# Attention, top-1 experts and a cosine layer in one kernel: a copy and a sum moved to ACT and POOL, sixteen weight loads moved ahead, ring slots renumbered

## The chip, the cores and the metric

One NeuronCore of a Trainium2 chip runs the whole program. The metric is the device time of one execution in microseconds (us). The engines are PE (matrix products), DVE, ACT and POOL (elementwise work), and SP, which here only issues transfers. PEld is the loading of PE's weights.

## The reference, cut to what matters

```python
def _attn_ref(q, k, v, g_norm):                    # 8 batches, 8 heads, 576 tokens, 64 wide
    kv = np.einsum('bhsd,bhse->bhde', k, v)
    out = np.einsum('bhsd,bhde->bhse', q, kv)
    rms = np.sqrt(np.mean(out * out, axis=-1, keepdims=True) + 1e-06)
    return (out / rms * g_norm).astype(np.float32)

def _moe_ref(x, expert_emb, tau, w1, w2):           # 4608 tokens x 512, 8 experts, hidden 1024
    ...                                             # one expert per token, gate_w its probability
    for e in range(E):
        h = np.maximum(x[mask] @ w1[e], 0.0)
        out[mask] = gate_w[mask, None] * (h @ w2[e])

def _moe2_ref(x, w_in, w_out):                      # 512 -> 2048 -> 512, weights in float64
    h = x @ w_in
    g = h * np.cos(h)
    return (g @ w_out).astype(np.float32)
```

## The kernel before

Every matrix product is made to float32's accuracy from three products of rounded parts: each operand is written as `hi` (a rounded copy, made by ACT) plus `lo` (the rest, made by DVE). The program has three stages, one after the other, and the order of the instructions on each engine is the order of the code.

**Attention** (0 to about 144 us) also finds each token's expert and scatters the tokens to DRAM by expert.

**Experts** (about 144 to 612 us). Tokens come in 16 chunks of 304, two an expert. A loop counts steps `g` from 0 to 129; step `g` is `c, f = divmod(g, 8)`: chunk `c`, eighth `f` of the hidden width. In a step PE does `layer1(c, f)` (L253) and `layer2` of two steps before (L274). Into the same steps other work is laid by hand:
- `split_piece` (L140 on ACT, L141 on DVE) turns an eighth of an expert's weights from `raw` into `hi` and `lo` in one of 12 ring slots. Which slot a piece gets is found by the loop at L101 to 107, and with it the earliest step for its split (`split_at`).
- `gate_x` works out the gates of a coming chunk in small DVE and ACT operations (L174 to L210, with four `gx` operations in step f = 3), and `turn_x` turns its tokens into `xT` (L227 on PE, L232 on ACT, L233 on DVE) in steps f = 3 to 6. A chunk's first `layer1` (f = 0) needs all four `xT`.
- `convert` turns the float64 weights of the last stage into float32, on DVE: four bit operations (L324 to L331), four sums (L455) and three splits (L365, to the tile `wa`, with copies by ACT, L364) for each set, 16 sets in all. How much of it goes into a step is a sum kept by hand: `spare` grows by `FULL` = 32 a step, less what `vector_work` counts of other work (12 for a split).

**The cosine layer** (about 602 us to the end). Nine blocks `b` of 512 tokens, eight steps each, `step(i)` with `b, q_ = divmod(i, 8)` for 256 hidden columns. A fast scheme of seven products instead of eight is used for both layers: a step has seven products of the first layer (`ha`, `hb`, L1124), whose sums (`one`, `five`, `two`) ACT copies and DVE adds up to `h`; the cosine and the parts of `h` made in the step before; and seven products of the second layer (L1137) with the `h` of two steps before, into the PSUM banks `a11`, `s2`, `a12`, `s3`, `a22`, `s1`. Weights of the first layer, and three of the second, are streamed by `feed` through nine slots (`wb`, `wa` and two in the ring), each load issued on SP when a product is done with a slot. The other four of the second layer (`KEPT`) stay in SBUF: those of q_ = 0 are in `wa` already, those of q_ = 1 to 7 are 28 loads made by `keep_one` (L533) into ring slots. Eight of them are issued at the end of the loop over the experts, the others one for every second `feed`.

In the first step after a block (`after` in `step`; eight times in the program) DVE sums the finished banks into the output tiles `o_sb`, of which `late_sum` does two out of bank `s1` (`o_s` in the trace), and POOL writes the rows out by token number (L1195). The first second-layer product of the new block that goes to bank `s1` is the last of that step.

Of the kernel before, what the change touches and what calls it, by code (L numbers as in the profile page):

```python
# [14 lines left out]
ALU = mybir.AluOpType  # L15
# [14 lines left out]
CH = 304  # L30
CP = 76
NRB = 12
# [4 lines left out]
def tile_kernel(ctx, tc, q, k, v, g_norm, emb, tau, w1, w2, w_in, w_out, out):  # L37
    nc = tc.nc
# [53 lines left out]
    NC = len(chunks)  # L92
# [7 lines left out]
    free_at = [-99] * 8 + [OPEN] * 4  # L100
    slot_of, earliest = [], []  # L101
    for p, (first, final) in enumerate(use):

        i = p - 4 if 12 <= p < 16 else min(range(NRB), key=lambda x: (free_at[x], x))
        slot_of.append(i)
        earliest.append(free_at[i] + 1)
        free_at[i] = final
# [35 lines left out]
    V = nc.vector  # L143
# [136 lines left out]
    def store_y(c):  # L280
        o = [P.yo.tile([128, CH], F32, name="yo", tag="yo") for _ in range(4)]
        for d in range(4):
            if "gate" in c:
                V.tensor_tensor(out=o[d], in0=c["y"][d][:, 0:CH], in1=c["gate"], op=ALU.mult)  # L284
            else:
                nc.scalar.activation(out=o[d], in_=c["y"][d][:, 0:CH], func=ACTF.Copy)

        def flush():
            by_pool = c["n"] < BY_POOL or c["n"] == NC - 1
            queue = nc.gpsimd if by_pool else nc.sync  # L290
            col = c["col"](mybir.EngineType.Pool if by_pool else mybir.EngineType.SP)
            queue.dma_start(out=perm[bass.ds(col, CH)].rearrange("(p r) -> p r", r=4), in_=c["rows"])
            for d in range(4):
                queue.dma_start(out=yT[d * 128:(d + 1) * 128, bass.ds(col, CH)], in_=o[d])

        return flush
# [189 lines left out]
    KEPT = (W11, W21, W22, V1)  # L486
# [42 lines left out]
    def keep_one():  # L529
        q_, j = keeping.pop(0)  # L530
        if j == 0:
            WOUT[q_] = ring(WO[q_ - 1])
        nc.sync.dma_start(  # L533
            out=WOUT[q_][:, :, j * 256:j * 256 + 256].bitcast(F32), in_=wo[q_, KEPT[j]].rearrange("p (a c) -> p a c", a=2)
        )
# [39 lines left out]
    if True:  # L575
# [62 lines left out]
        for i in range(2):  # L638
# [6 lines left out]
            out=ident, in_=ones, pattern=[[1, 128]], compare_op=ALU.is_equal, fill=0.0, base=0, channel_multiplier=-1  # L645
        )
        nc.gpsimd.affine_select(
            out=upper, in_=ones, pattern=[[1, 128]], compare_op=ALU.is_gt, fill=0.0, base=0, channel_multiplier=-1
# [11 lines left out]
        for i in range(2):  # L660
            nc.gpsimd.iota(
                out=nums[64 * i:64 * i + 64, :, 8], pattern=[[2 * S, 4]], base=i * S + 512, channel_multiplier=1
# [322 lines left out]
        for t in range(NTILE):  # L985
            j, b, r = where(t)
# [60 lines left out]
    if True:  # L1047
# [55 lines left out]
        G, Y, bank = {}, {}, {}  # L1103
# [61 lines left out]
        def copy(out, in_):  # L1165
            nc.scalar.activation(out=out, in_=in_, func=ACTF.Copy)  # L1166

        def add(out, x, y):
            V.tensor_tensor(out=out, in0=x, in1=y, op=ALU.add)  # L1169

        def sub(out, x, y):
            V.tensor_tensor(out=out, in0=x, in1=y, op=ALU.subtract)  # L1172

        def f32(x):
            return x.bitcast(F32)
# [26 lines left out]
        def halves(x):  # L1202
            return x.rearrange("p (t c) -> p t c", t=2)

        OUT = {}
# [10 lines left out]
            return p.tile([128, 512], F32, name=name, tag=name)[:, 0:256]  # L1216

        def late_sum(b, t, x):
            add(OUT[b][t][:, :, 256:512], halves(x), halves(bank[b, "s1"]))
            for th in range(2):  # L1220
                out_row(b, t, th)

# [35 lines left out]
        def step(i):  # L1258
            if i == NS + 1:
                return last_step()  # L1260
            new, prev, j = i < NS, 1 <= i <= NS, i - 2
            last = i - 1
            b, q_ = divmod(j, 8)
            done = j >= 0 and q_ == 7
            after = j >= 8 and q_ == 0
# [11 lines left out]
            def o(kind="o"):  # L1277
                return out_product(pe(kind)) if j >= 0 else None

            if new:  # L1280
                xa = bank_of("ha", i)
                xb = bank_of("hb", i)
                if i:
                    h1, h0 = (hp_.tile([128, 512], F32, name="h", tag="h") for _ in range(2))
                    one, five, two = (sn.tile([128, 256], F32, name=nm, tag=nm) for nm in ("one", "five", "two"))
# [5 lines left out]
            else:  # L1291
                xa = xb = None
# [43 lines left out]
            if prev:  # L1336
                sub(s24[:, 1], r0[:, 1], s24[:, 0])
                copy(hi0, r0)
                copy(hi13, s13)
                copy(hi24, s24)  # L1340
                sub(lo0, r0, f32(hi0))
            if after:
                add(OUT[b - 1][1][:, :, 0:256], halves(E1), halves(bank[b - 1, "a22"]))
# [3 lines left out]
            if not i:  # L1347
                interleave(1)
            o()
            if prev:  # L1350
                sub(lo13, s13, f32(hi13))
            if new:
                add(h1[:, 256:512], five, xa)
                turns_of(i, 1)
            if done:
                add(U2, E1, bank[b, "s2"])
            if after:
                late_sum(b - 1, 1, E1)
            if new:
                xb = bank_of("hb", i)  # L1360
            h(xb, True)
# [6 lines left out]
            if done:  # L1368
                OUT[b] = [op.tile([128, 2, 512], F32, name=f"o_sb{t}", tag=f"o_sb{t}") for t in range(2)]
                add(OUT[b][0][:, :, 0:256], halves(E1), halves(bank[b, "a12"]))  # L1370
            if after:
                late_sum(b - 1, 0, Y["acc"])
            if prev:
                sub(lo24, s24, f32(hi24))
            if new:
# [30 lines left out]
        for n in range(5, NC):  # L1406
            GATE_AT[8 * n - 14] = LOAD_AT[8 * n - 17] = n
        raw_of = lambda: P.raw.tile([128, 1024], F32, name="raw", tag="raw")
        spare, FULL, CARRY = 0, 32, 15

        def vector_work(c, f, splits):
            w = 4 + 12 * splits + (6 if c >= NC - 2 else 14 if c == 2 else 0) + (16 if f == 1 and c < 5 else 0)
# [4 lines left out]
        for g in range(NC * 8 + LAG):  # L1417
# [41 lines left out]
            if g == 8 * NC - 5:  # L1459
                feed()  # L1460
                feed()
            if 8 * NC - 1 <= g < 8 * NC + 1:
                for _ in KEPT:
                    keep_one()
            if g < OPEN:
                paused.clear()
                advance(8)
# [240 lines left out]
```

## Time and profile before

| what | value |
|---|---|
| median of 3 runs | 1357.23 us (1357.14 to 1366.95) |
| the profiled execution, its own time | 1357.04 us |
| its span, first to last instruction | 1355.5 us |
| busy in the span | PE 1302.9 us (96%), DVE 1102.2 (81%), ACT 846.2 (62%), POOL 175.4 (13%) |
| moved by DMA | 359.31 MB, mean 265 GB/s |
| mean granted TensorE clock | 0.995 |

The 1.5 us between span and time lie outside the first and last instruction. A busy share is a mean over stages: in most slices of the span PE is busy without a gap, and its idle time lies in the attention stage, at the passage from one stage to the next, and in short waits between.

### The profile page before, as it was taken

The numbers are of one execution on the slowest core, as the hardware profiler recorded it, in microseconds if no ns is written. First come the engines' busy times: TensorE is split into PE (matmuls) and PEld (weight loads), VectorE is DVE, ScalarE is ACT, GpSimd is POOL, SyncE is SP. The second block draws the span as 40 slices with busy tenths as digits, with TensorE's granted clock in tenths as the row PEclk, the third lists the DMA queues.
The fourth block names the chain that finished last, engine by engine and source line by source line (L and its number), as shares of the span: only waits on it lengthen the run. The fifth ranks groups of instructions, "written<-read, shape, count | busy, mean of one in ns | idle before, by whom it ended". The sixth has DMA issues, their size and how long they took to land.

```text
span 1355.5 us, 30321 instructions
## 1 busy us (share of the span) xinstructions
PE 1302.9 (96%) x10825; PEld 1279.5 (94%) x10825; DVE 1102.2 (81%) x2511; ACT 846.2 (62%) x1698; POOL 175.4 (13%) x286
## 2 busy tenths in 40 slices
PE   7998799999999999998999999999999999999997
PEld 6886799999999999998999999999999999999997
DVE  2567867788989888866889898888989889798876
ACT  4667454677666776545666666676666766666663
POOL 1234132113220000000001010000101001010101
PEclk9999999999999999999999999999999999999998
DMA  9999485788888798659998888888889889888884
GB/s 276 290 326 284 133 246 129 209 249 261 251 249 272 253 281 274 211 163 329 339 320 296 284 293 269 290 285 299 284 267 309 271 290 294 284 291 271 262 284 136
DMA packets 238102, 359.31 MB, mean 265 GB/s; under 512 B 26045, under 2 KB 114913, under 8 KB 236729
## 3 DMA queue, kind: packets, MB, share of 16 engines
q1 hardware_dynamic: 221480, 297.20, 69.3%
q0 software_dynamic: 16448, 60.08, 14.0%
q8 instruction: 89, 1.46, 0.4%
q14 instruction: 69, 0.56, 0.1%
q10 hardware_dynamic: 16, 0.02, 0.0%
HBM read 299.32 MB, written 57.89 MB: 264 GB/s over the span
## 4 chain that ended last, share of the span: by engine, by line
PE 66%; DVE 11%; issue 9%; DMA 5%; ACT 4%; SPq 3%; POOL 1%; POOLq 0%; ACTq 0%; DVEq 0%
PE ha L1124 12%; PE y L274 10%; PE hb L1124 9%; PE o_s L1137 9%; PE o_a L1137 9%; PE hps L253 7%; PE hb L1137 3%; PE xp L253 3%; DMA vr<-in_v 1%; DMA wa<-ws 1%; SPq L599 1%; DVE gx L180 1%; DVE ring L141 1%; DVE o_sb L1169 1%; ACT gx L174 1%
## 5 line engine op out<-in xcount | busy, mean ns | idle before, releaser
L274 PE MATMUL y<-h,ring 128*128 128x304 f32 x1536 | 235.8, 302 | 1.3 <-DVE yo L284 1.3
L274 PEld LDWEIGHTS y<-h,ring 128*128 128x128 f32 x1536 | 220.1, 188 | 1.7 <-ACT h L259 1.5
L253 PE MATMUL hps<-xT,ring 128*128 128x304 f32 x1152 | 182.8, 308 | 2.7 <-DVE xT L233 1.8
L253 PEld LDWEIGHTS hps<-xT,ring 128*128 128x128 f32 x1152 | 165.0, 190 | 4.1 <-DVE xT L233 2.2
L1092 ACT ACTIVATE u<-u,half_pi 128x512 f32<-128x512 f32 x142 | 102.3, 720 | 56.8 <-DVE u L1089 56.8
L1195 POOL DMA_INDIRECT out<-o_sb,perm_i x36 | 48.6, 1350 | 684.8 <-DVE o_sb L1169 576.5
L1086 ACT ACTIVATE u<-h 128x512 int32<-128x512 f32 x142 | 89.7, 632 | 71.0 <-DVE h L1169 65.0
L1089 DVE SCALAR_TENSOR_TENSOR u<-h,u 128x512 f32<-128x512 f32 x142 | 97.9, 689 | 24.8 <-ACT u L1086 22.9
L1137 PE MATMUL o_a<-ring,hi 128*128 128x256 f32 x568 | 107.9, 282 | 0.0
L141 DVE TENSOR_TENSOR ring<-raw,ring 128x1024 fp32r<-128x1024 f32 x72 | 87.8, 1219 | 21.3 <-ACT ring L140 20.6
L1166 ACT ACTIVATE hi<-u 128x512 fp32r<-128x512 f32 x142 | 88.6, 624 | 26.5 <-DVE u L1172 26.5
L1172 DVE TENSOR_TENSOR lo<-u,hi 128x512 fp32r<-128x512 f32 x142 | 96.9, 683 | 0.0
L259 ACT ACTIVATE h<-hps 128x304 fp32r<-128x304 f32 x96 | 40.3, 419 | 78.6 <-PE hps L253 74.5
L1137 PEld LDWEIGHTS o_a<-ring,hi 128*128 128x128 f32 x568 | 87.2, 189 | 0.0
L1166 ACT ACTIVATE hi<-h 128x256 fp32r<-128x256 f32 (+1 forms) x142 | 74.2, 522 | 19.6 <-PE o_a L1137 9.1
L1325 DVE TENSOR_TENSOR h<-h,u 128x512 f32<-128x512 f32 x71 | 49.0, 690 | 44.5 <-ACT u L1092 44.1
L1137 PE MATMUL o_a<-ring,lo 128*128 128x256 f32 x284 | 79.7, 281 | 0.0
L1172 DVE TENSOR_TENSOR lo<-h,hi 128x256 fp32r<-128x256 f32 (+1 forms) x142 | 78.2, 550 | 0.0
L140 ACT ACTIVATE ring<-raw 128x1024 fp32r<-128x1024 f32 x72 | 75.8, 1053 | 0.0
L1137 PE MATMUL o_s<-ring,hi 128*128 128x256 f32 x376 | 71.9, 283 | 0.0
L253 PE MATMUL xp<-xT,ring 128*128 128x304 f32 x384 | 60.1, 303 | 2.4 <-DVE xT L233 2.4
L260 DVE SCALAR_TENSOR_TENSOR h<-hps,h 128x304 fp32r<-128x304 f32 x96 | 44.4, 463 | 18.2 <-ACT h L259 16.3
(333 smaller groups left out, 3374.2 us busy)
## 6 DMA issues: line engine op xcount, KB each, us to landing
wb<-ws SPq DMA_DIRECT2D x224, 256.0 KB
wa<-ws SPq DMA_DIRECT2D x167, 256.0 KB
raw<-in_moe_w SPq DMA_DIRECT2D x144, 256.0 KB
ring<-ws SPq DMA_DIRECT2D x113, 256.0 KB
wb<-wo SPq DMA_DIRECT2D x96, 256.0 KB
ring<-wo SPq DMA_DIRECT2D x75, 256.0 KB
wa<-wo SPq DMA_DIRECT2D x73, 256.0 KB
wo<-wa SPq DMA_DIRECT2D x52, 256.0 KB
```

The source lines that it names most:

```text
L140: nc.scalar.activation(out=w[:, 0], in_=raw, func=ACTF.Copy)
L141: nc.vector.tensor_tensor(out=w[:, 1], in0=raw, in1=w[:, 0].bitcast(F32), op=ALU.subtract)
L253: nc.tensor.matmul(out=p[:, 0:CH], lhsT=w[:, a, k * 128:(k + 1) * 128], rhs=c["xT"][b_][k], start=(n == 0), stop=(n == 11),)
L274: nc.tensor.matmul(out=c["y"][d][:, 0:CH], lhsT=w[:, a, 512 + d * 128:512 + (d + 1) * 128], rhs=h[b_], start=(f == 0 and i == 0), stop=(f ...
L1086: nc.scalar.activation(out=n, in_=p, func=ACTF.Copy, scale=TURN, bias=0.25)
L1089: V.scalar_tensor_tensor(out=u, in0=p, scalar=TURN, in1=n, op0=ALU.mult, op1=ALU.subtract)
L1092: nc.scalar.activation(out=u, in_=u, func=ACTF.Sin, scale=2 * math.pi, bias=half_pi)
L1124: nc.tensor.matmul(out=out, lhsT=w[:, a, k * 128:(k + 1) * 128], rhs=x[xi][:, b_, k * 256:(k + 1) * 256], start=(start and n == 0), stop=( ...
L1137: nc.tensor.matmul(out=o[:, th * 256:th * 256 + 256], lhsT=G[j, name][a][:, th * 128:th * 128 + 128], rhs=w[:, b_, 0:256], start=(start an ...
L1166: nc.scalar.activation(out=out, in_=in_, func=ACTF.Copy)
L1172: V.tensor_tensor(out=out, in0=x, in1=y, op=ALU.subtract)
L1325: V.tensor_tensor(out=r0, in0=r0, in1=two_of(Y["u", 0]), op=ALU.mult)
```

## The change

It has six parts:
1. **Ring slots.** Pieces 16 to 23 get slots 0 to 7. Their splits move: pieces 16 to 21 from steps 14, 16, 18, 20, 22, 24 to 19, 21, 22, 23, 24, 25; from piece 22 on the steps are as before. The last expert's pieces lie in slots 0 to 7 instead of 4 to 7 and 0 to 3.
2. **`FULL`** goes from 32 to 33.
3. **Kept weights.** Sixteen of the 28 loads (q_ = 1 to 4) are issued in steps 124, 125 and 126, instead of eight in steps 127 and 128; the other twelve stay with the feeds.
4. **Last chunk's output.** Of its four copies out of PSUM ACT keeps two, and DVE does two.
5. **Order of two DVE operations** in every step: `h1[:, 256:512]` is added ahead of the split `lo13`.
6. **`late_sum`.** ACT copies bank `s1` to `U2` behind `hi24`, and POOL adds `U2` for both output halves (`E1` and `Y["acc"]`), both in the place of the first; DVE no longer does these two sums.

```diff
-        i = p - 4 if 12 <= p < 16 else min(range(NRB), key=lambda x: (free_at[x], x))
+        i = p - 4 if 12 <= p < 16 else p - 16 if 16 <= p < 24 else min(range(NRB), key=lambda x: (free_at[x], x))
...
             if "gate" in c:
                 V.tensor_tensor(out=o[d], in0=c["y"][d][:, 0:CH], in1=c["gate"], op=ALU.mult)
+            elif c["n"] == NC - 1 and d % 2:
+                V.tensor_copy(out=o[d], in_=c["y"][d][:, 0:CH])
             else:
...
         def late_sum(b, t, x):
-            add(OUT[b][t][:, :, 256:512], halves(x), halves(bank[b, "s1"]))
+            nc.gpsimd.tensor_tensor(out=OUT[b][t][:, :, 256:512], in0=halves(x), in1=halves(U2), op=ALU.add)
             for th in range(2):
                 out_row(b, t, th)
...
                 copy(hi24, s24)
+                if after:
+                    copy(U2, bank[b - 1, "s1"])
                 sub(lo0, r0, f32(hi0))
...
+            if new:
+                add(h1[:, 256:512], five, xa)
             if prev:
                 sub(lo13, s13, f32(hi13))
             if new:
-                add(h1[:, 256:512], five, xa)
                 turns_of(i, 1)
             if done:
                 add(U2, E1, bank[b, "s2"])
             if after:
                 late_sum(b - 1, 1, E1)
+                late_sum(b - 1, 0, Y["acc"])
...
-            if after:
-                late_sum(b - 1, 0, Y["acc"])
...
-        spare, FULL, CARRY = 0, 32, 15
+        spare, FULL, CARRY = 0, 33, 15
...
-            if 8 * NC - 1 <= g < 8 * NC + 1:
-                for _ in KEPT:
-                    keep_one()
+            for _ in range({8 * NC - 4: 8, 8 * NC - 3: 4, 8 * NC - 2: 4}.get(g, 0)):
+                keep_one()
```

Three places show how instructions move. First SP at the passage from the experts to the cosine layer (steps 124 to 129), where loads from `ws` and those from `wo` into `wb` and `wa` are feeds, and the loads from `wo` into a numbered `ring` of 128x2x256 are kept weights. Before:

```order
L517 DMA wa<-ws 128x512 x3
L517 DMA ring_8090<-ws 128x512 x2
L533 DMA ring_8563<-wo 128x2x256
L517 DMA wb<-ws 128x512 x2
L533 DMA ring_8563<-wo 128x2x256
L517 DMA wb<-ws 128x512 x2
L533 DMA ring_8563<-wo 128x2x256
L517 DMA wa<-ws 128x512
L533 DMA ring_8563<-wo 128x2x256
L533 DMA ring_8671<-wo 128x2x256 x4
L533 DMA ring_8676<-wo 128x2x256 x3
L517 DMA wa<-ws 128x512 x2
```

And now, from the same three feeds on:

```order
L519 DMA wa<-ws 128x512 x3
L535 DMA ring_8464<-wo 128x2x256 x4
L535 DMA ring_8469<-wo 128x2x256 x4
L535 DMA ring_8503<-wo 128x2x256 x4
L535 DMA ring_8542<-wo 128x2x256 x4
L519 DMA ring_8097<-ws 128x512 x2
L519 DMA wb<-ws 128x512 x4
L519 DMA wa<-ws 128x512 x3
```

All sixteen stand ahead of the feeds of step 0 (two in the ring, four in `wb`, one in `wa`), and nothing stands between these and the next feeds to `wa`.

Second DVE in the first step after the first block (`o_sb` are output tiles, `o_s` the bank `s1`, `e` is `E1`; `u` and `h` the parts of the hidden layer). Before:

```order
L1172 TENSOR_TENSOR lo_10063<-h,hi_10062 128x512
L1169 TENSOR_TENSOR o_sb_10008<-e_8724,o_a_8955 128x2x256
L1172 TENSOR_TENSOR lo_10067<-u_9987,hi_10066 128x512
L1169 TENSOR_TENSOR h<-five,ha 128x256
L1169 TENSOR_TENSOR o_sb_10008<-e_8724,o_s_8965 128x2x256
L1169 TENSOR_TENSOR h<-one,hb 128x256
L1089 SCALAR_TENSOR_TENSOR u_10149<-h,u_10149 128x512
L1169 TENSOR_TENSOR o_sb_10007<-acc,o_s_8965 128x2x256
L1172 TENSOR_TENSOR lo_10069<-u_10049,hi_10068 128x512
L1188 TENSOR_TENSOR h<-h,u_10149 128x512
```

And now:

```order
L1174 TENSOR_TENSOR lo_10063<-h,hi_10062 128x512
L1171 TENSOR_TENSOR o_sb_10008<-e_8730,o_a_8960 128x2x256
L1171 TENSOR_TENSOR h<-five,ha 128x256
L1174 TENSOR_TENSOR lo_10067<-u_9987,hi_10066 128x512
L1171 TENSOR_TENSOR h<-one,hb 128x256
L1091 SCALAR_TENSOR_TENSOR u_10150<-h,u_10150 128x512
L1174 TENSOR_TENSOR lo_10069<-u_10049,hi_10068 128x512
L1190 TENSOR_TENSOR h<-h,u_10150 128x512
```

The two sums out of `o_s` are gone from DVE (POOL does them now, each in front of its two row writes), and the split of 128x512 stands behind the sum to `h` instead of in front of it.

Third DVE in steps 57 and 58 of the experts (`sb` and `sa` are the sums of the conversion, `wa` its splits). Before:

```order
L141 TENSOR_TENSOR ring_5119<-raw,ring_5119 128x1024
L326 SCALAR_TENSOR_TENSOR c_t<-c_raw,c_t 128x512
L329 SCALAR_TENSOR_TENSOR c_t<-c_raw,c_t 128x512
L331 SCALAR_TENSOR_TENSOR sa<-c_mk,c_t 128x512
L260 SCALAR_TENSOR_TENSOR h_5144<-xp,h_5143 128x304
L455 TENSOR_TENSOR sb<-sa 128x256
L455 TENSOR_TENSOR sa<-sa 128x256
L455 TENSOR_TENSOR sb<-sb,sa 128x256
L455 TENSOR_TENSOR sb<-sa,sb 128x256
```

And now:

```order
L141 TENSOR_TENSOR ring_5128<-raw,ring_5128 128x1024
L457 TENSOR_TENSOR sb<-sb,sa 128x256
L457 TENSOR_TENSOR sb<-sa,sb 128x256
L260 SCALAR_TENSOR_TENSOR h_5151<-xp,h_5150 128x304
L367 TENSOR_TENSOR wa<-sa,wa 128x2x256 x2
L367 TENSOR_TENSOR wa<-sb,wa 128x3x256
```

The conversion runs some operations ahead of where it ran, so its three splits, which need three copies by ACT, now fall into step 58 (f = 2) instead of step 60.

## Rows read from the trace of the kernel before

**Rows 1.** Waits of PE over the whole span: total us, how often, longest.
```profile
PE o_s L1137 <- DVE o_sb L1169: 4.0, 8, 0.5
PE xp L253 <- DVE xT L233: 2.4, 4, 0.7
```

**Rows 2.** Stretches: length, busy us (instructions) of PE, PEld, DVE, ACT, POOL, clock, DMA share, GB/s.
```profile
600.00:610.00 10.00, 10.00 (x80) 10.00 (x79) 3.42 (x7) 2.88 (x7) 0.00 (x0) 1.00 0.57 175
620.00:630.00 10.00, 7.36 (x50) 7.19 (x49) 6.61 (x14) 5.47 (x12) 0.00 (x0) 0.83 1.04 362
```

**Rows 3.** PE at the passage, in order of time: start, us, what, idle before and releaser.
```profile
614.63 0.98 PE L1124 MATMUL ha<-ring,ring 128*128 128x256 f32 x6 [1.04 <-ACT one L1166]
...
618.79 0.98 PE L1124 MATMUL ha<-ring,wb 128*128 128x256 f32 x6 [0.89 <-DVE h L1169]
...
624.55 1.20 PE L1124 MATMUL o_s<-ring,wa 128*128 128x256 f32 x6 [2.64 <-DMA wa<-ws]
...
635.19 0.95 PE L1124 MATMUL hb<-ring,wa 128*128 128x256 f32 x6 [0.79 <-DMA wa<-ws]
```

**Rows 4.** SP's queue at the passage, in order of time.
```profile
610.46 6.28 SPq L533 DMA_DIRECT2D ring<-wo  x8
616.85 1.45 SPq L517 DMA_DIRECT2D wa<-ws  x2
```

**Rows 5.** ACT and DVE at the passage, in order of time.
```profile
612.66 1.34 ACT L286 ACTIVATE yo<-y 128x304 f32<-128x304 f32 x4
617.11 1.29 DVE L1172 TENSOR_TENSOR lo<-raw,hi 128x512 fp32r<-128x512 f32 x2
622.03 0.36 ACT L1166 ACTIVATE one<-o_s 128x256 f32<-128x256 f32 x1
```

**Rows 6.** The second block's end and the step behind it, in order of time.
```profile
795.91 0.63 ACT L1086 ACTIVATE u<-h 128x512 int32<-128x512 f32 x1 [1.50 <-DVE h L1169]
...
800.62 0.36 ACT L1166 ACTIVATE one<-ha 128x256 f32<-128x256 f32 x1
...
801.03 0.98 PE L1124 MATMUL ha<-ring,wa 128*128 128x256 f32 x6
...
803.79 0.41 DVE L1169 TENSOR_TENSOR h<-two,hb 128x256 f32<-128x256 f32 x1
...
804.70 0.88 PE L1124 MATMUL hb<-ring,ring 128*128 128x256 f32 x6
```

**Rows 7.** POOL's elementwise sums, grouped by form over the whole span.
```profile
L878 POOL TENSOR_TENSOR exc<-exc,ohc 128x8 f32<-128x8 f32 x16 | 3.3, 209 | 6.9 <-DVE ohc L873 6.3
...
L865 POOL TENSOR_TENSOR w<-w,tie 128x24 f32<-128x24 f32 x8 | 2.0, 254 | 32.7 <-DVE w L864 32.6
```

**Rows 8.** DVE and POOL at 117 us, in order of time.
```profile
117.20 1.21 DVE L141 TENSOR_TENSOR ring<-raw,ring 128x1024 fp32r<-128x1024 f32 x1
117.28 1.20 POOL L879 TENSOR_TENSOR run<-exc,ohc 128x8 f32<-128x8 f32 x1
```

**Rows 9.** Experts: splits in steps 43 and 51, first products of steps 48 and 56.
```profile
308.73 1.23 DVE L141 TENSOR_TENSOR ring<-raw,ring 128x1024 fp32r<-128x1024 f32 x1 [0.47 <-ACT ring L140]
...
320.52 1.56 PE L253 MATMUL xp<-xT,ring 128*128 128x304 f32 x10
...
322.70 0.54 PE L253 MATMUL xp<-xT,ring 128*128 128x304 f32 x2 [0.63 <-DVE xT L233]
...
336.38 1.23 DVE L141 TENSOR_TENSOR ring<-raw,ring 128x1024 fp32r<-128x1024 f32 x1 [0.47 <-ACT ring L140]
...
349.43 1.94 PE L253 MATMUL xp<-xT,ring 128*128 128x304 f32 x12
...
399.70 0.69 DVE L326 SCALAR_TENSOR_TENSOR c_t<-c_raw,c_t 128x512 int32<-128x512 int32 x1
```

**Rows 10.** The split of step 14 on DVE, and PE's wait for a gate behind it.
```profile
202.05 1.22 DVE L141 TENSOR_TENSOR ring<-raw,ring 128x1024 fp32r<-128x1024 f32 x1 [0.37 <-ACT ring L140]
...
215.18 1.92 PE L274 MATMUL y<-h,ring 128*128 128x304 f32 x12 [1.29 <-DVE yo L284]
```

## The prediction, made before the changed kernel ran

> **What bounds the kernel now.** I began with the table of engines and went on to the list of waits. PE is busy 1302.9 of 1355.5 us, so nothing here pays unless it takes away an idle moment of PE, a stretch of low clock, or adds one. The list of waits by sum [rows 1] names two that the change touches: eight at the block boundaries of the cosine layer, 4.0 us in all, in which the last product of a step waits for DVE to empty bank `s1`, and four at the start of an expert's chunk, 2.4 us. The timeline adds four waits at the passage from the experts to the cosine layer [rows 3], 1.04 + 0.89 + 2.64 + 0.79 = 5.36 us, and the table of stretches shows there a granted clock of 0.83 for 10 us [rows 2]: PE had been held up just before, and the chip granted only part of full speed. One more wait, 1.29 us, lies early in the experts [rows 10]. All together about 15 us stand within reach, 1.1% of the time. The page's sum is made against the profiled execution, 1357.04 us; the median is 0.2 us above it, which I neglect.
>
> **Passage (parts 3, 4 and 5).**
> - *Last chunk's output.* ACT makes four copies in 1.34 us [rows 5], and the first of `ha` waits 1.04 us for the copy `one` queued behind them [rows 3]. With two left, ACT is done 1.34 / 2 = 0.67 us sooner: −0.67. DVE's two copies take what ACT's take, about 0.67 us, in front of splits that PE needs only several microseconds later; at nothing, and at most 0.67 if that cover fails.
> - *Order of sum and split.* The 0.89 us wait is for the sum `h` on DVE, in front of which two splits take 1.29 us [rows 3, 5]. One of the two is now behind it: −1.29 / 2 = −0.64. The split that is put back has its user two products later; in steady steps I cost it at nothing, since the splits of a step are used in the next.
> - *Kept loads.* SP spends 6.28 us issuing eight kept loads at 610.46, and only then, at 616.85, the feeds to `wa` that PE waits for until 624.55 [rows 3, 4]. After the change no kept load stands there (the first pair of lists), so these feeds go out when their slots come free. PE is ready at 624.55 − 2.64 = 621.91; the next thing it needs, ACT's copy `one`, ends at 622.03 + 0.36 = 622.39 [rows 5], 0.5 us late. So −2.64 + 0.5 = −2.1. The wait of 0.79 at 635.19 is a load in the same backlog, in which the DMA engines were full (1.04 between 620 and 630 [rows 2]); I take it as gone: −0.79. With PE not held up I let the clock stay at full speed: −(1 − 0.83) × 10 = −1.7.
> - *What the moved loads pass.* Sixteen loads of 128x2x256 floats, 262 KB each, 4.2 MB in all, now stand on SP ahead of the first feeds of step 0. A step of the experts takes (349.43 − 320.52) / 8 = 3.6 us [rows 9], so steps 124 to 126 lie some 20 us ahead of 612 and the loads go out between about 590 and 602. Their issue takes twice 6.28 = 12.6 us. The cover is that step 0 needs its feeds only from about 614 and that the DMA engines between 600 and 610 are 0.57 busy [rows 2]: at 362 GB/s, the rate of the full stretch, 4.2 MB take 11.6 us, of which the spare 0.43 leaves room by 620 for more than half. Cost nothing; if the cover is gone, the waits stay (rival C).
>
> Sum of the passage: −0.67 − 0.64 − 2.1 − 0.79 − 1.7 = −5.9; bounds −7.1 (all waits and the clock) and −1.3 (only the first two).
>
> **Early experts (part 1).** In step 14 DVE makes a split of 1.22 us after 0.37 us of waiting for ACT; a gate of the next chunk is made behind it, and PE waits 1.29 us for it at 215.18 [rows 10]. The split goes to step 19, so 1.22 to 1.6 us of DVE's time are freed ahead of the gate, as much as the wait: −1.3. The splits of steps 19 to 25 come closer together, where nothing in PE's waits names them; bound 0.
>
> **Conversion (part 2).** One unit more a step brings the conversion forward. The four waits of [rows 1] on `xT` lie where the three wide splits, with their three ACT copies, fall in f = 1 or 2 of the chunk before: there the split of f = 3 starts at 308.73, 11.8 us ahead of the next chunk's first product at 320.52, and PE waits 0.63; in the chunk after, it starts 13.05 us ahead of 349.43, and there is no wait [rows 9]. The lists of the changed kernel put those splits in f = 1 or 2 in steps 41, 58, 81 and 98, again four chunks. In the chunks that begin at steps 64 and 104 DVE has about one conversion operation more in f = 4 to 6; nearest for its length is the split of 1.23 us less half its width, 0.6 to 0.7. So two waits near 0.6, as before, and two near 1.4: 4.0 against 2.4, +1.7 with rounding and a short wait at step 80. Bounds 0 (the positions make no difference) and +4 (every one of the four like the worst).
>
> **Block boundaries (part 6).** What leaves: eight waits, −4.0 [rows 1]. ACT has the room, 1.50 us idle ahead of `u` at 795.91 [rows 6], so the copy of `s1`, of the kind that takes 0.6 us, is done at about 795.1, and PE wants the bank at about 797.6. What arrives: two sums of 128x512 on POOL. The trace has no such form. The nearest rows are sums of 128x8 in 209 ns and 128x24 in 254 ns [rows 7]: 45 ns for 16 elements, 2.8 ns each, so 0.2 + 512 × 2.8 ns = 1.6 us, an estimate. What they do to DVE is shown once [rows 8]: a POOL sum began 0.08 us after a DVE split with two inputs in SBUF, lasted 1.20 us instead of some 0.25, and ended within 0.1 us of it. One of the two stood still. Who stands still when POOL is first, no row shows. Here POOL is first: its sum starts at about 795.1, DVE's split with two inputs at 795.3. If DVE then waits for the rest of the sum, it loses 1.35 us; the two sums that it no longer makes cost it 0.68 each, 1.36. So DVE's product, the parts of `h`, and ACT's copy `one` stay where they were. `one` ends at 800.62 + 0.36 = 800.98 and PE starts at 801.03 [rows 6], 0.05 us of slack, so the 0.5 us that PE gains at `s1` it then waits for `one`. Net per boundary 0; bounds −0.5 (DVE not held) and the loss of rival B. I take 0, by the row of contention, the only one there is.
>
> The Trainium skill, page GPSIMD Engine Reference, section 3.1 (Elementwise — side-by-side cycle accounting), puts a two-input sum at some 2.6 cycles an element against DVE's 1; by it, with the 2048-element sum that the page gives as 4497 ns, a sum of 512 would take an estimated 1.1 us, and rival B would give 1356.3 rather than 1360.3. No row here shows such a length, and the sum does not use it.
>
> **Forecast:** 1357.04 − 5.9 − 1.3 + 1.7 + 0 = 1351.5 us.
>
> **Rivals.**
> - *A: POOL costs DVE nothing that PE waits for.* For it: DVE gets 1.36 us back at each boundary, and much of what follows there reads one operand from PSUM. Against it: [rows 8]. All eight waits go: 1351.5 − 4.0 = 1347.5.
> - *B, slower: POOL holds DVE for the whole of both sums.* The first costs what DVE saved. The second stands on POOL behind two row writes, and starts some 3.6 us after the first ends, at about 800.3; nothing was taken off DVE there. DVE's `h` from `two` and `hb` ends at 803.79 + 0.41 = 804.20, and PE needs it at 804.70 [rows 6]: 0.5 us of slack. A hold of 1.6 us gives a wait of 1.1, eight times: +8.8, so 1360.3, more than before; up to 1364 if the first hold too exceeds the saving by 0.5. The point that decides is a hold longer than 0.5 us in that second place. For it: [rows 8], with the roles exchanged. Against: POOL's sum may fall between DVE's operations.
>   The Trainium skill, SBUF — State Buffer, section "Who interferes with whom", states this outright: a DVE instruction with two SBUF inputs contends with a GpSimd instruction that reads SBUF, and whichever is issued first has the shared ports for its whole instruction. By that rule the time is B's; the trace agrees for the order DVE first [rows 8], and shows nothing for the other.
> - *C: the change does not do what it says at the passage.* The sixteen loads are still in the queues when step 0's feeds are issued, and PE waits for them as it did. For it: 12.6 us of issue ahead of those feeds, and full DMA engines from 620 on [rows 2, 4]. The last three terms of the passage stay: 1351.5 + 2.1 + 0.79 + 1.7 = 1356.1.
>
> **How the numbers follow.** Forecast 0.35, A 0.30, B 0.20, C 0.15. The lowest that I hold likely is A with the conversion at its bound of 0, 1345.8; the range starts at 1346. Above, it takes in C and the first price of B: 1361. A difference under 1%, 13.6 us, a measurement of this kernel can hardly tell from none; that means 1343.5 to 1370.8 here. Faster than that needs nearly every wait in reach and the clock: 0.06, from the edge of A. Slower needs B half as dear again: 0.04. Within: 0.90.
>
> **What would show it.** At the passage: waits of about 0.4 and 0.25 us on ACT's `one` and DVE's `h`, no wait on a load of `wa`, a clock near 1.0 from 620 to 630 (C if not). At the boundaries: no wait on `o_s`, and its length moved to `one` in the next step (forecast), nowhere (A), or more than a microsecond on DVE's `h` before `hb` (B); the length of POOL's sums and of DVE's operations beside them. In the experts: no wait at about 215, longer ones at steps 64 and 104. The prediction is wrong above all if POOL's sums are much longer than 1.6 us, if a steady step of the cosine layer grows by the exchange of sum and split (a tenth of a microsecond there is 7 us over 72 steps), or if the earlier loads hold up the experts' own weights.

## The result, and the profile after

The changed kernel is slower: the ratio to the kernel before is 1.0054, with a 95% interval of 1.0039 to 1.0069 (medians of 20 runs 1366.38 and 1360.42 us, 6.0 apart; further runs of the kernel before moved its median up from the three shown). Forecast was 1351.5 us in a range of 1346 to 1361. The profiled execution has a span of 1364.3 us against 1355.5: 8.8 us more; that of the kernel before is one of its faster ones (1357.04 us). So the prediction failed in its sign, though not everywhere.

The list of waits of the changed kernel; its columns are who waited in which line for whom, total us, how often, longest.

```profile
PE ha L1126 <- ACT one L1168: 8.3, 8, 1.1
PE ha L1126 <- issue: 6.9, 7, 1.0
...
PE xp L253 <- DVE xT L233: 3.8, 4, 1.6
...
PE ha L1126 <- ACT u L1094: 1.0, 1, 1.0
PE hb L1126 <- DMA wb<-ws: 0.9, 2, 0.7
```

The eight waits on bank `s1` [rows 1] are gone, as the change says. In their place `ha` waits: eight times at the first product of the step that follows (6.9 + 1.0 us; for seven of them the profile finds no releaser, for one it names ACT's cosine), and seven times about 1.1 us for `one` at the third product of that step (the eighth of that line is the passage's 0.46). Let us first see the parts that went as forecast.

**Passage.** PE from the changed kernel's timeline, to be held against [rows 3], and two stretches against [rows 2]:

```profile
614.43 0.98 PE L1126 MATMUL ha<-ring,ring 128*128 128x256 f32 x6 [0.46 <-ACT one L1168]
...
617.98 0.98 PE L1126 MATMUL ha<-ring,wb 128*128 128x256 f32 x6 [0.29 <-DVE h L1171]
...
621.78 0.98 PE L1126 MATMUL o_s<-ring,wa 128*128 128x256 f32 x6 [0.67 <-ACT one L1168]
```

```profile
600.00:610.00 10.00, 10.00 (x80) 10.00 (x79) 3.79 (x8) 2.90 (x7) 0.00 (x0) 1.00 1.10 350
...
620.00:630.00 10.00, 8.96 (x73) 8.56 (x72) 8.71 (x18) 7.34 (x16) 0.00 (x0) 1.00 1.02 356
```

The load of `wa` is no longer waited for, what is late next is `one`, by 0.67, and the clock stays at 1.00. The DMA engines are full from 600 on (1.10, where it was 0.57), while PE is busy without a gap, and still at 1.02 between 620 and 630.

**Block boundary.** DVE, POOL and ACT behind the first block, where POOL now makes the sums to `o_sb`:

```profile
707.72 0.58 ACT L1168 ACTIVATE u<-o_s 128x512 f32<-128x512 f32 x1
708.21 0.41 DVE L1171 TENSOR_TENSOR h<-five,ha 128x256 f32<-128x256 f32 x1
708.39 1.28 POOL L1221 TENSOR_TENSOR o_sb<-e,u 128x512 f32<-128x512 f32 x1 [91.87 <-ACT u L1168]
708.54 1.68 DVE L1174 TENSOR_TENSOR lo<-u,hi 128x512 fp32r<-128x512 f32 x1
...
710.14 0.41 DVE L1171 TENSOR_TENSOR h<-one,hb 128x256 f32<-128x256 f32 x1
710.25 0.63 ACT L1088 ACTIVATE u<-h 128x512 int32<-128x512 f32 x1 [1.95 <-DVE lo L1174]
...
712.27 0.36 ACT L1168 ACTIVATE h<-ha 128x256 f32<-128x256 f32 x1
712.40 1.97 DVE L1190 TENSOR_TENSOR h<-h,u 128x512 f32<-128x512 f32 x1 [0.19 <-ACT u L1094]
712.50 1.31 POOL L1221 TENSOR_TENSOR o_sb<-acc,u 128x512 f32<-128x512 f32 x1
...
712.69 0.98 PE L1126 MATMUL ha<-xb,wb 128*128 128x256 f32 x6 [0.96 <-ACT u L1094]
...
716.24 0.97 PE L1126 MATMUL ha<-xb,wa 128*128 128x256 f32 x6 [1.15 <-ACT one L1168]
```

Two DVE operations that take 0.68 and 0.69 us undisturbed take 1.68 and 1.97: 1.00 and 1.28 more (1.68 to 1.69 and 1.93 to 1.97 at all eight boundaries). The first begins 0.15 us after the POOL sum and ends 0.55 after it: it stood still until the sum had ended, and then ran its own 0.68 (records may overlap by 0.1). The second is written down 0.1 us ahead of its POOL sum and was held all the same. `h<-five,ha`, with one operand in PSUM, was running when the first sum began, and kept its 0.41. Follow the first hold on: the split ends at 710.22, ACT's `u` waits for that split and starts at 710.25, and ACT, which goes on from there to the cosine, comes to its copy out of `ha` at 712.27; PE starts at 712.69 when that copy is done, 0.96 us late. The second hits DVE's product with the cosine, and so the copy `one` behind it, 1.15 us.

From boundary to boundary the kernel before needs 566.87 / 7 = 80.98 us (1284.03 against 717.16, the eighth and the first wait on `o_s`), the changed one 578.92 / 7 = 82.70 (1291.61 against 712.69); 0.66 of the whole is a late load of `wb`. Without it that is 1.6 us a boundary.

### The profile page after: what moved, and what is told of

It reads as the page before. It is cut to its first block, busy times and chain, and to the rows that moved or that the text cites. A ratio compares the mean times of both kernels' runs of the same rounds, so it can differ in the third digit from the quotient of the medians.

```text
span 1364.3 us, 30299 instructions
## 1 busy us (share of the span) xinstructions
PE 1306.2 (96%) x10825; PEld 1281.7 (94%) x10825; DVE 1111.9 (82%) x2497; ACT 850.5 (62%) x1704; POOL 187.7 (14%) x302
## 5 line engine op out<-in xcount | busy, mean ns | idle before, releaser
L1174 DVE TENSOR_TENSOR lo<-u,hi 128x512 fp32r<-128x512 f32 x142 | 105.2, 742 | 0.0
L1221 POOL TENSOR_TENSOR o_sb<-e,u 128x512 f32<-128x512 f32 x8 | 10.3, 1284 | 614.1 <-ACT u L1168 614.1
L1327 DVE TENSOR_TENSOR h<-h,u 128x512 f32<-128x512 f32 x71 | 49.0, 690 | 44.8 <-ACT u L1094 43.6
L1190 DVE TENSOR_TENSOR h<-h,u 128x512 f32<-128x512 f32 x71 | 59.1, 833 | 12.0 <-ACT u L1094 10.7
```

The costliest lines, as they stand in the source:

```text
L1190: V.tensor_tensor(out=Y[j, t], in0=Y[j, t], in1=Y["u", t], op=ALU.mult)
L1327: V.tensor_tensor(out=r0, in0=r0, in1=two_of(Y["u", 0]), op=ALU.mult)
```

## The experiments

All times are spans of the profiled execution; each ratio is to the kernel before, on the same chip. The attention stage ends between about 143 and 150 us from one execution to the next, so spans alone differ by some microseconds, and the kernels are told apart by the ratios and by their waits.

**e1: the sums back on DVE, ACT's copy kept.**

```diff
         def late_sum(b, t, x):
-            nc.gpsimd.tensor_tensor(out=OUT[b][t][:, :, 256:512], in0=halves(x), in1=halves(U2), op=ALU.add)
+            add(OUT[b][t][:, :, 256:512], halves(x), halves(U2))
...
                 late_sum(b - 1, 1, E1)
-                late_sum(b - 1, 0, Y["acc"])
...
+            if after:
+                late_sum(b - 1, 0, Y["acc"])
             if prev:
                 sub(lo24, s24, f32(hi24))
```

> The changed kernel with ACT's copy of bank s1 kept, but its two sums made by DVE out of the copy, in the places where DVE made them before. Theory T (a POOL sum holds back DVE operations with two inputs in SBUF for as long as it runs): the two waits of 0.96 and 1.15 us a boundary go; the wait at the bank stays gone; at most 0.5 us a boundary comes back as a wait on ACT's copy one. Span 1347 to 1352 against 1364.3 of the changed kernel. Rival R (ACT's added copy, or the exchange of sum and split, delays the cosine chain): the waits of about 2.1 us a boundary stay, span 1362 to 1366.

Span 1356.1, but its experts began 4.9 us later than the changed kernel's (149.33 against 144.43), so 1351 from an equal start; ratio 0.9967 (0.9954 to 0.998). Of the waits at a boundary 0.19 to 0.20 on `one` is left, at seven of the eight, and at three of them 0.15 on a copy of ACT:

```profile
721.74 0.97 PE L1126 MATMUL ha<-xb,wa 128*128 128x256 f32 x6 [0.19 <-ACT one L1168]
```

ACT's copy and the exchange of sum and split stand as in the changed kernel, so rival R falls.

**e2: part 6 alone undone.** The calls of `late_sum` stand as in e1, and

```diff
-            nc.gpsimd.tensor_tensor(out=OUT[b][t][:, :, 256:512], in0=halves(x), in1=halves(U2), op=ALU.add)
+            add(OUT[b][t][:, :, 256:512], halves(x), halves(bank[b, "s1"]))
...
-                if after:
-                    copy(U2, bank[b - 1, "s1"])
```

> Part 6 alone undone: no copy of s1, both sums on DVE out of the bank, as before; parts 1 to 5 kept. Theory T: eight waits of 0.5 us on the bank come back, the waits of 2.1 us go: span 1364.3 - 8 x 1.62 = 1351.3, and the kernel is faster than before by about 0.3%. Rival R': part of the loss lies in parts 1 to 5 (conversion, kept loads): span above 1355.

Span 1351.5, ratio 0.9964 (0.9951 to 0.9978). The eight waits on the bank are back, and none on `one` is left in the cosine layer after the passage:

```profile
PE o_s L1139 <- DVE o_sb L1171: 4.1, 8, 0.6
```

Parts 1 to 5 together are a gain, and part 6 the whole of the loss. Part 5, the exchange of sum and split, costs nothing here: from the first wait on `o_s` to the eighth a block takes (1279.84 − 714.04) / 7 = 80.83 us, against 80.98 in the kernel before.

**e3: each POOL sum in four pieces.**

```diff
         def late_sum(b, t, x):
-            nc.gpsimd.tensor_tensor(out=OUT[b][t][:, :, 256:512], in0=halves(x), in1=halves(U2), op=ALU.add)
+            for th in range(2):
+                for y in (0, 128):
+                    nc.gpsimd.tensor_tensor(
+                        out=OUT[b][t][:, th, 256 + y:384 + y], in0=x[:, 256 * th + y:256 * th + y + 128],
+                        in1=U2[:, 256 * th + y:256 * th + y + 128], op=ALU.add,
+                    )
```

> The changed kernel with each POOL sum cut into four pieces of 128x128, everything else the same. Theory T, in the form that the hold lasts for one instruction: a DVE operation is held for at most one piece, about 0.5 us, not for the rest of 1.3 us; the sums lengthen to about 4 x 0.5 us; waits a boundary fall from 2.1 to 1.0 to 1.6 us; span 1356 to 1361. Rival (POOL and DVE share a rate, whatever the instructions' length): DVE loses as much or more, since POOL works longer; span 1364 or above.

Span 1357.2, but this is the fastest of ten executions (their median time is 1365.35 us, near the rival's bound); ratio 1.0033 (1.0015 to 1.0052). What decides is the trace. DVE and POOL behind the first block:

```profile
707.52 2.17 POOL L1223 TENSOR_TENSOR o_sb<-e,u 128x128 f32<-128x128 f32 x4 [92.67 <-ACT u L1168]
707.67 0.86 DVE L1174 TENSOR_TENSOR lo<-u,hi 128x512 fp32r<-128x512 f32 x1
708.45 0.41 DVE L1171 TENSOR_TENSOR h<-one,hb 128x256 f32<-128x256 f32 x1
...
709.23 1.01 DVE L1091 SCALAR_TENSOR_TENSOR u<-h,u 128x512 f32<-128x512 f32 x1 [0.37 <-ACT u L1088]
...
712.63 2.72 POOL L1223 TENSOR_TENSOR o_sb<-acc,u 128x128 f32<-128x128 f32 x4
```

The split that lost 1.00 loses 0.18 now, `u` 0.32: no operation is held for longer than a piece, and `h<-one,hb`, with one operand in PSUM, runs its 0.41 right beside them. The hold belongs to the instruction. POOL's own work has grown from 1.28 to 2.17 and 2.72, since it now waits for DVE as well, and more of DVE's operations are held a little; a boundary costs PE 0.47 + 0.86 = 1.3 us instead of 2.1.

**e4: the sums on DVE, the second a step later.** `late_sum` as in e1; then

```diff
             if after:
-                late_sum(b - 1, 1, E1)
                 late_sum(b - 1, 0, Y["acc"])
...
+            if j >= 8 and q_ == 1:
+                late_sum(b - 1, 1, E1)
             if j >= 0 and q_ % 2:
                 t = o("t")
```

> ACT's copy of s1 kept; DVE makes both sums out of the copy, the one from acc in the step after the block, the one from E1 a step later, where DVE has 0.93 us of idle time ahead of the turns. Theory T: no wait on the bank, none on one: 8 x 2.1 = 17 us less than the changed kernel, span about 1347, and faster than before by about 0.6%. If the later place delays the parts of h there, up to 0.7 us a boundary stays: 1353.

Span 1348.9, ratio 0.9945 (0.9929 to 0.996): faster than both kernels. Of the boundaries three waits of 0.15 to 0.17 are left, and the later sum lies where DVE had waited 0.93 us for ACT (the changed kernel's 724.87):

```profile
723.33 0.69 DVE L1190 TENSOR_TENSOR h<-h,u 128x512 f32<-128x512 f32 x1 [0.19 <-ACT u L1094]
723.94 0.69 DVE L1171 TENSOR_TENSOR o_sb<-e,u 128x512 f32<-128x512 f32 x1
724.61 0.69 DVE L1091 SCALAR_TENSOR_TENSOR u<-h,u 128x512 f32<-128x512 f32 x1
```

**e5 and e8: e4 with the experts' parts undone**, the old ring slots and `FULL` = 32 in e5, the old slots alone in e8.

```diff
-        i = p - 4 if 12 <= p < 16 else p - 16 if 16 <= p < 24 else min(range(NRB), key=lambda x: (free_at[x], x))
+        i = p - 4 if 12 <= p < 16 else min(range(NRB), key=lambda x: (free_at[x], x))
...
-        spare, FULL, CARRY = 0, 33, 15
+        spare, FULL, CARRY = 0, 32, 15
```

> e4_spread with parts 1 and 2 undone (ring slots and FULL = 32 as before). If the conversion's place sets the waits at the chunks' starts, they go from 3.8 back to 2.4 us, at steps 48, 72, 88 and 112, about 0.6 each, and the wait of 1.0 to 1.3 us for a gate at about 215 stays or comes back to 1.3: the experts' length 1.4 us less, at most 0.2 back: span about 1.2 us below e4_spread's apart from the attention's own spread. If parts 1 and 2 together are worth something, it is 1 us longer.

> e4_spread with part 1 alone undone: the old ring slots, FULL = 33 kept. If the split in step 14 delays a gate, the wait at about 215 us is 1.3 us or more, against 1.1 in e4_spread; the chunk waits stay at about 3.8, as the conversion runs as in e4_spread from step 41 on. Prediction's size for part 1 was 1.3 us; the runs so far leave 0.2 to 0.8.

Spans 1359.8 and 1363.5, ratios 1.0023 (1.0008 to 1.0039) and 1.0035 (1.0017 to 1.0054): e5 misses its expected span by about 12 us, and e8, for which only waits were expected, is slower still. The loss is not in the experts. There the waits came as expected: in e5 the four go back to 0.63, 0.55, 0.72 and 0.47 (2.4 us), in e8 they stay at 0.69, 1.54, 0.45 and 1.26, and the wait for the gate is 1.79 and 1.45 (each has one more wait on `xT`, of 0.54 and 0.38, at about 209 us). All waits of that kind are 2.9 us in e5 and 4.3 in e8, which differ in `FULL` alone, so part 2 loses 1.4 us there too. The larger loss is at the passage; SP and PE in e8, with what SP waited for:

```profile
606.14 15.38 SPq L535 DMA_DIRECT2D ring<-wo  x16
...
621.57 1.90 SPq L519 DMA_DIRECT2D ring<-ws  x2
...
628.46 1.62 PE L1126 MATMUL ha<-ring,ring 128*128 128x256 f32 x6 [9.21 <-DMA ring<-ws]
```

```profile
SPq L535 <- PE y L274: 10.3, 3, 5.8
```

And the changed kernel, whose experts began 3.5 us earlier:

```profile
594.34 11.99 SPq L535 DMA_DIRECT2D ring<-wo  x16
606.61 1.08 SPq L519 DMA_DIRECT2D ring<-ws  x2
```

With the old slots SP waits with the sixteen loads 10.3 us (three times, for products `y`) until the last expert's pieces have left the slots, and the feeds of step 0 wait in the same queue; PE stands for 9.21 us, and the granted clock is 0.63 between 620 and 630. So part 1 is what makes part 3 possible. I had read it as a matter of one gate.

**e6: e4 with part 3 undone.**

```diff
-            for _ in range({8 * NC - 4: 8, 8 * NC - 3: 4, 8 * NC - 2: 4}.get(g, 0)):
-                keep_one()
+            if 8 * NC - 1 <= g < 8 * NC + 1:
+                for _ in KEPT:
+                    keep_one()
```

> e4_spread with part 3 undone: eight kept loads at the passage as before. The prediction's reading: PE waits about 2 us or more for a feed to wa again, the clock falls below 1 in the stretch behind it, and the stretch from the first ha to the end of the first block is 4 to 5 us longer. Rival: the loads of the feeds are late anyway, since the queues are full; then it is less than 1.5 us longer.

Span 1355.8, ratio 0.9975 (0.9961 to 0.9989). PE waits for the feed again, and the clock is 0.90 between 620 and 630, 0.93 in the next 10 us:

```profile
628.52 1.62 PE L1126 MATMUL o_s<-ring,wa 128*128 128x256 f32 x6 [2.84 <-DMA wa<-ws]
```

From the first `ha` (616.96; 612.94 in e4) to the same wait on `wa` some 65 us later, where both stand again, it takes 67.60 us against 64.41: 3.2 us longer. That is nearer to the reading than to its rival, but less than the 4 to 5 expected.

**e7: POOL writes, but reads nothing.** The kernel leaves out the two sums of each boundary.

```diff
-            nc.gpsimd.tensor_tensor(out=OUT[b][t][:, :, 256:512], in0=halves(x), in1=halves(U2), op=ALU.add)
+            nc.gpsimd.memset(OUT[b][t][:, :, 256:512], 0.0)
```

> The changed kernel with each POOL sum replaced by a POOL memset of the same half of the output tile, which reads nothing; the sums are left out. Theory T (what holds DVE is POOL's reading of SBUF beside a DVE operation with two SBUF inputs): DVE's operations beside it keep 0.68 us, both waits of a boundary go, span about 1364.3 - 8 x 2.1 = 1347. Rival (any work of POOL on SBUF holds DVE): each hold shortens to the memset's length, some 0.5 us, and a wait of 0.2 to 1 us a boundary stays, span 1350 to 1357.

Span 1348.3, ratio 0.9943 (0.9924 to 0.9962): no wait at any boundary. Behind the second block:

```profile
794.34 0.69 DVE L1190 TENSOR_TENSOR h<-h,u 128x512 f32<-128x512 f32 x1 [0.19 <-ACT u L1094]
...
794.39 0.55 POOL L1221 MEMSET o_sb<- 128x512 f32 x1
...
799.04 0.53 POOL L1221 MEMSET o_sb<- 128x512 f32 x1 [1.55 <-DMA out<-o_sb,perm_i]
799.08 0.42 DVE L1174 TENSOR_TENSOR u<-h 128x256 f32<-128x256 f32 x1
```

The same product of DVE with two inputs in SBUF that a sum had held for 1.28 us runs its 0.69 beside a writing POOL. A memset is shorter than a sum, but a hold of even 0.55 would show here, and there is none. Only the second memset of a boundary stands in the place of its sum; the first need not wait for ACT's copy and runs some 70 us earlier. The one at 799.04 is such a first one: it begins ahead of a DVE operation with two inputs in SBUF, which keeps its 0.42.

**e9: one sum on POOL, the other on DVE.**

```diff
         def late_sum(b, t, x):
-            nc.gpsimd.tensor_tensor(out=OUT[b][t][:, :, 256:512], in0=halves(x), in1=halves(U2), op=ALU.add)
+            if t:
+                nc.gpsimd.tensor_tensor(out=OUT[b][t][:, :, 256:512], in0=halves(x), in1=halves(U2), op=ALU.add)
+            else:
+                add(OUT[b][t][:, :, 256:512], halves(x), halves(U2))
```

(the second call stands where it stands in e1)

> The changed kernel with only the first sum (from E1) left on POOL; the second (from acc) made by DVE out of the copy, where DVE made it before. Theory T says what each sum costs: the first holds the split of 128x512 for 1.0 us, so the wait of about 0.96 us at the step's last ha stays; in place of the second hold of 1.29 us DVE has 0.68 us of work of its own, so the wait on one falls from 1.15 to about 0.5. Span 1364.3 - 8 x 0.6 = 1359.5. The prediction's reading (the first hold is paid for by the sums that DVE no longer makes, so it costs nothing): the wait at ha is gone, span below 1354.

Span 1359.6, but from a start 4.5 us later; ratio 1.0008 (0.9992 to 1.0024). At each boundary 0.95 to 1.00 us at the first `ha` of the next step, as with both sums, and about 0.2 on `one` instead of 1.15 (0.5 expected):

```profile
717.14 0.98 PE L1126 MATMUL ha<-xb,wb 128*128 128x256 f32 x6 [0.97 <-ACT h L1168]
...
719.74 0.97 PE L1126 MATMUL ha<-xb,wa 128*128 128x256 f32 x6 [0.19 <-ACT one L1168]
```

Each sum costs PE about 1 us by itself. The first is not paid for by what DVE no longer does, which is what the prediction had taken.

**e10: e4 with the conversion further ahead.**

```diff
-        spare, FULL, CARRY = 0, 33, 15
+        spare, FULL, CARRY = 0, 44, 15
```

> e4_spread with FULL = 44: the conversion runs further ahead, and its three wide splits fall in f = 1 or 2 of a chunk in three steps (49, 74, 89) instead of four (41, 58, 81, 98). If that place is what makes a chunk's first product wait for xT, the waits lie at steps 56, 80 and 96 and at no other chunk, 1.5 to 3.5 us in all against 3.8. If the load of DVE a step is what counts, they grow, since more of the conversion stands in each step, and others appear on h and yo.

Span 1387.8, ratio 1.0199 (1.0174 to 1.0224). All eight chunks from step 48 to step 104 wait for `xT`, 11.0 us in all, and a gate made late costs 9.79:

```profile
PE xp L253 <- DVE xT L233: 11.0, 8, 1.7
PE y L274 <- DVE yo L284: 9.8, 1, 9.8
```

The place of the wide splits is not the whole rule for these waits: how much of the conversion stands in a step counts too. How the two share the 3.8 us of the changed kernel stays open; no run separates them.

## Why the prediction was wrong

**The step that failed** is the one that closes the block boundaries: "If DVE then waits for the rest of the sum, it loses 1.35 us; the two sums that it no longer makes cost it 0.68 each, 1.36. So DVE's product, the parts of `h`, and ACT's copy `one` stay where they were." The hold was read rightly, from [rows 8]: a sum of 1.28 to 1.31 us (forecast 1.6) that held a DVE operation for 1.00 (forecast 1.35). The balance was wrong, because time on DVE is not worth the same everywhere. The held split stands ahead of ACT's `u`, and from there a chain over ACT and DVE leads to the copy of `ha`; the sums taken off DVE had stood behind that split, where they could give nothing back to it. Before, `u` began at 795.91 behind `h<-five,ha` [rows 6]; now it begins behind the held split. e9 shows this sum's price alone, about 0.97 us a boundary. One thing stays open: no run has the sums on POOL and the old order of sum and split. In that order the split would have stood where `h<-five,ha` is now, at 708.21, ahead of the POOL sum at 708.39, so the first hold may hang on parts 5 and 6 together.

**Rival B** named the other half: the second sum, behind two row writes, holding DVE in a chain without slack. It did: 1.28 us, and a wait of 1.15 (priced 1.1), but that the two are so near is luck: the hold was 0.3 shorter than the 1.6 taken, and the slack 0.1 instead of 0.5. The wait came on `one` in the next step and not on `h` before `hb`, and about 4.1 us after the start of the first sum, where B had 3.6 after its end. B added nothing for the first sum except in its upper price, 1364. At a boundary the sums cost 0.96 + 1.15 - 0.49 = 1.62 us, and 1.6 × 8 = 13 us would be the whole. Seven boundaries took that, and the last less: 0.95 at the first product, and no wait listed on `one`.

The Trainium skill, SBUF — State Buffer, section "Who interferes with whom", had said it: a DVE instruction with two SBUF inputs contends with a GpSimd instruction that reads SBUF, not with one that only writes it, the first of the two has the shared ports for its whole instruction, and a DVE instruction with at most one SBUF input, outside its two-port modes, does not contend. The runs agree in each: 1.00 and 1.28 us of hold beside POOL's sums, no operation with one SBUF input held (0.41 in e3), and none held beside a memset (e7); the two-port modes no run here shows. The estimate of 1.1 us from the Trainium skill, GPSIMD Engine Reference, section 3.1, was nearer to the measured 1.28 than mine of 1.6 from two short forms.

**What came as forecast.** Passage: −5.9 us forecast. From the first `ha` to the same later wait on `wa` the kernel before takes 680.98 − 611.99 = 68.99 us, the changed one 675.46 − 612.39 = 63.07: −5.9. In its terms: 1.04 to 0.46 and 0.89 to 0.29 (−1.18, forecast −1.31), 2.64 gone and 0.67 in its place (−1.97, forecast −2.1), 0.79 gone; about 2.0 remain, which fits the clock, 1.00 instead of 0.83 (forecast −1.7). e6, with part 3 alone undone, gives 3.2 for that part, against 4.6 in the forecast. Conversion: four waits of 0.59, 1.56, 0.44 and 1.20 at steps 48, 64, 88 and 104, 3.8 us against 2.4: +1.4, forecast +1.7, in the steps named; only the short wait at step 80 did not come. Rival C fell with the clock, and A with the boundaries.

**Where a size was off.** The gate's wait, forecast to go (−1.3), is at 0.48 us in the changed kernel, but between 0.60 and 1.30 in the seven runs whose experts are the same up to there (e1 to e4, e6, e7, e9). The mean of these eight is 0.9 us; with the old slots it was 1.29, 1.79 and 1.45 (before, e5, e8), 1.5 in the mean: 0.6 gained, not 1.3. The gate is made 1.4 us earlier (205.53 instead of 206.94), as forecast, but it goes to DRAM and back before DVE can use it (the first three lines are from before):

```profile
206.94 0.17 DVE L205 RECIPROCAL gt<-y 76x4 f32<-76x4 f32 x1
...
209.31 0.56 POOL L219 DMA_DIRECT2D gate<-gates  x1 [1.36 <-DMA gates<-gt]
...
214.56 1.62 DVE L284 TENSOR_TENSOR yo<-y,gate 128x304 f32<-128x304 f32 x4 [1.23 <-DMA gate<-gates]
```

```profile
205.53 0.17 DVE L205 RECIPROCAL gt<-y 76x4 f32<-76x4 f32 x1
...
207.92 0.56 POOL L219 DMA_DIRECT2D gate<-gates  x1 [1.38 <-DMA gates<-gt]
...
213.84 1.62 DVE L284 TENSOR_TENSOR yo<-y,gate 128x304 f32<-128x304 f32 x4 [2.02 <-DMA gate<-gates]
```

In the changed kernel it is 5.9 us from POOL's second issue to `yo` (213.84 − 207.92); before it was 5.3 (214.56 − 209.31). The experts as a whole (from their first product to the first `ha`) take 467.96 us against 467.94: the +1.4 of the conversion, −0.8 at the gate, and −0.65 for a wait on `xT` at 232.07 that was not in the forecast and is gone. The prediction also took a difference under 1% for one that can hardly be told from none; here 0.54% was told, with an interval of 0.39 to 0.69%.

The sum of the profiled execution: +0.4 start of the experts, 0 experts, −6.2 from the first `ha` to the end of the first block (98.46 us against 104.68), about +12.4 boundaries, +0.7 a late load of `wb` at 858, and about +1.5 at the end, most of it the landing of the last row writes (8.5 us from issue to the end against 7.2), which part 6 does not touch. That is 8.8.

## What to carry to other kernels

Before a sum is handed to POOL, look which DVE operations will run beside it, and how many of their operands lie in SBUF: with two, DVE stood still here until POOL's sum had ended, and what counts is who waits behind the held operation, not how much work DVE has been rid of. The useful half of such a change may be the early copy, but not by itself: with it and both sums on DVE in their old places (e1, 0.9967) nothing is gained over leaving part 6 out (e2, 0.9964). It paid, though little, when one of the sums went a step later, to an idle place (e4, 0.9945: its interval just overlaps that of e2, but the eight waits on the bank, 4.1 us, are gone). And a load that is moved ahead in SP's queue needs its slot free there, or what stands behind it waits as well (e8); undo a renumbering of slots only together with what relies on it.

## What the runs showed that I had not expected

- DVE's product in the second place was held although its record starts 0.1 us ahead of POOL's: the start of a record does not tell who was first.
- Sums cut into four pieces lengthen from 1.28 to 2.17 and 2.72 us, and take the waits of a boundary from 2.1 to 1.3 us only.
- In e8 PE stood from 619.25 to 628.46; the granted clock, 1.00 before, was 0.63 between 620 and 630, and still 0.86 in the next 10 us.
